# First layer of the token threes as 3x3 by 3x4 block products (29 of two units for 15 of four), and the threes' work issued in a list scheduler's order

## The chip, the cores and the metric

The kernel runs on one core of a Trainium2 chip. The metric is device time in microseconds: the median of several executions of the whole program.

## The reference

Sigmoid attention over 8 batches, 12 heads, 448 positions and head size 64, and then a feed-forward net with a squared ReLU over all 3584 tokens. All of it is float32.

```python
scores = scale * np.matmul(q, k.transpose(0, 1, 3, 2)) - np.log(S)
attn = 1.0 / (1.0 + np.exp(-scores))
x = np.matmul(attn, v)          # -> 3584 tokens x 768
h = x @ w_in                    # 768 x 2048
r = np.maximum(h, 0.0)
g = s * (r * r) + b
out = g @ w_out                 # 2048 x 768
```

## The kernel before

**Numbers.** Every matrix operand is split into a high part (rounded by ScalarE, `hi`) and a low part (the remainder, by VectorE, `lo`). A product is then three matmuls: high by high, high by low, low by high (`PARTS`).

**Three stages.** (1) Attention; beside it the weights of both layers are loaded as raw words and converted on VectorE and ScalarE, and the row sums of the first weight tiles of layer 2 are made. (2) *Token block 0* (512 of the 3584 tokens) goes through the net in the plain way, one tile of 128 hidden units after another (`order`: tiles 0, 8, 1, 9, ... 7, 15, sixteen iterations). Iteration i issues `ffn1` of its tile on TensorE, then the split of the next tile's weights (`base`), some of the weight sums, the activation (`activate`: four ScalarE operations, then the low part `g` on VectorE), and `ffn2` of the tile before it. So TensorE sees ffn1(i), ffn2(i-1), ffn1(i+1), ffn2(i), ..., and after the last ffn1 two ffn2 in a row. (3) The other six token blocks are taken in two *threes* of three blocks.

**The threes.** In a three, both layers are block matrix products computed with fewer multiplications than the plain way, from sums of blocks. Layer 1 multiplies 3 token blocks x 3 parts of the model width by 3 parts x 2 halves of the hidden width: 15 products instead of 18. Each product covers half the hidden width, as four *units* of 256 hidden columns; a unit is 12 matmuls of 128x512 (`L1095`). So layer 1 has 60 units per three, 720 matmuls, and layer 2 (`L1225`), also 15 products of four units, again 720. A product needs one operand from the tokens (`s_`, a sum of token tiles `a`, split into high and low on ScalarE and VectorE) and one *row* of the weights (a sum of weight blocks, split, stored in DRAM in `wd` during stage 2 and read back as `wu`, 512 KB for a unit). Results add up in four PSUM pairs or leave through ScalarE copies and VectorE additions.

**Row sums for layer 1** are made in stage 2 by `sums` (two row-sum groups of one hidden tile in each second iteration, eight sets of ten sums) and `sums_d`.

**Order.** Each engine runs its instructions in program order. All DMAs but two are issued by SyncE (SP) on one queue, in program order too. In the threes the order was written out by hand: tables `places`, `CHAINS_1`, `ORDER_2`, `early_jobs` and the due times `LATER_SUMS` say after which unit each sum, split and load is issued. The token tiles of the first three are loaded at the end of stage 2 in the order of `start`: 00, 20, 21 first, then 22 and 02, and the other four after the units 0 to 3.

**Memory.** Token sums, operands, results and hidden values live in equal 512 KB tiles, *slots*, of one heap (`Slots`): a freed slot goes to the back of a list and the next tile takes the one in front, so an instruction that fills a tile waits for the last reader of the slot's former content. Weight tiles wait in a roll of seven (`ROLL`).

Of the kernel before, what the change touches and what calls it, by code (L numbers as in the profile page):

```python
# [11 lines left out]
F32 = mybir.dt.float32  # L12
# [27 lines left out]
AHEAD = 6  # L40
# [5 lines left out]
LATER_SUMS = {  # L46
# [4 lines left out]
}  # L51
# [7 lines left out]
    (  # L59
# [4 lines left out]
    ),  # L64
    (
# [4 lines left out]
    ),  # L70
)

ROWS = (
    ("p", "q", "r", "u", "v", "w", "x", "y", "z", "d", "00", "10", "20", "01", "11"),
# [3 lines left out]
FIRST = {  # L78
# [3 lines left out]
}  # L82
SECOND = {
# [3 lines left out]
}  # L87

CHAINS_1 = ((4, 3), (10, 13, 2), (1, 8, 12), (7, 9, 11), (5, 0), (6, 14))
CHAINS_2 = ((8, 6, 7), (13, 10), (1, 5), (2, 4, 12), (3, 14, 9), (11, 0))  # L90
ORDER_2 = (8, 13, 6, 10, 7, 1, 2, 3, 5, 4, 11, 12, 14, 0, 9)
# [3 lines left out]
def sigmoid_attention_relu2_ffn(  # L95
# [19 lines left out]
    NPP = NP // 2  # L115
    NT = B * S // TB
# [14 lines left out]
    class Slots:  # L131


        def __init__(self, pl, n, tag):
            self.free_ = [(pl, f"{tag}{i}") for i in range(n)]
            self.at = {}

        def more(self, pl, n, tag):
            self.free_ += [(pl, f"{tag}{i}") for i in range(n)]

        def tile(self, shape, dtype, name):
            pl, tag = self.free_.pop(0)
# [4 lines left out]
        def free(self, t):  # L147
            _, pl, tag = self.at.pop(id(t))
            self.free_.append((pl, tag))
# [18 lines left out]
        [dram.tile([P, len(ROWS[l]), 2, 2 * KW], F32, name=f"wd_{l}_{p}") for p in range(NPP)]  # L168
        for l in range(2)
# [20 lines left out]
    for f in order:  # L190
        wf_tile(1, f, wfp_last if f % NP == NP - 1 else wfp)
        if f % NP < NP - 1:
            wf_tile(0, f, wfp)
# [27 lines left out]
    def block(l, f, n):  # L221

        third, hf = (int(n[0]), int(n[1])) if l == 0 else (int(n[1]), int(n[0]))
        return wf[l][f + hf * NP][:, third]
# [4 lines left out]
    def sums_ops(l, f, tl):  # L229
# [6 lines left out]
        def make(g):  # L236
            t = ts[g] = tl.tile([P, 3, 2, KW], F32R, name=f"t_{l}_{f}_{g}")
            k = 0
            for n, x, sign, y in SUMS[l][g]:
# [18 lines left out]
        def lo(g):  # L258
# [3 lines left out]
            def store():  # L262
# [4 lines left out]
                tl.free(t)  # L267

            if l:
                stores.append(store)  # L270
            else:
                store()
# [3 lines left out]
    def sums(l, f, tl):  # L276

        make, hi, lo = sums_ops(l, f, tl)
        make(0)
        make(1)  # L280
        yield
        hi(0)
        hi(1)
        yield
        make(2)
        lo(0)
        lo(1)
        yield
        hi(2)
        yield  # L290
        lo(2)
        yield

    def sums_d(l, p, tl):

        _, x, sign, y = SUMS[l][3]
# [7 lines left out]
        nc.sync.dma_start(wd[l][p][:, 9], f32(t).rearrange("p j h c -> p j (h c)"))  # L304
        tl.free(t)
# [11 lines left out]
    def base(l, f, t=None):  # L317
# [3 lines left out]
        hf, f = divmod(f, NP)  # L321
        thirds = [k for k in range(3) if (f"{k}{hf}" if l == 0 else f"{hf}{k}") in ROWS[l]]
        k0, k1 = thirds[0], thirds[-1] + 1
        row = ROWS[l].index(f"{k0}{hf}" if l == 0 else f"{hf}{k0}")
        nc.sync.dma_start(
            wd[l][f // 2][:, row : row + k1 - k0, f % 2],
            f32(t[:, k0:k1]).rearrange("p k h c -> p k (h c)"),
        )
        return t
# [157 lines left out]
    stores = []  # L487

# [163 lines left out]
    grps = ((0, 1), (2, 3))  # L652
    L1 = [(i, p) for c in CHAINS_1 for gr in grps for i in c for p in gr]
    L2 = [(i, p) for i in ORDER_2 for p in range(NPP)]
    stream = [(n, l, i, p) for n in range(len(threes)) for l in range(2) for i, p in (L1, L2)[l]]
    fetched = []

    def fetch():
        if len(fetched) < len(stream):
            n, l, i, p = stream[len(fetched)]  # L660
            t = roll.tile([P, 2, 2, KW], F32R, tag="wu", name=f"wu_{n}_{l}_{i}_{p}")
# [628 lines left out]
```

## Time and profile before

| | us |
|---|---|
| median of 3 runs (1038.56 to 1039.0) | 1038.66 |
| span of the profiled execution, first to last instruction | 1037.2 |
| TensorE matmuls busy | 1033.5 |
| VectorE busy | 837.3 |
| ScalarE busy | 617.0 |
| stage 1 / stage 2 / first three / second three, by the TensorE chain | 250.5 / 130.9 / 326.4 / 326.5 |

The profiled execution has no total of its own beside its span; the median of the runs lies 1.5 us above that span, which is the time around the first and the last instruction. The groups of the profile are read as: line, engine, operation, output<-input, shapes and count, then busy time, mean of one in ns, and the idle time of the engine just before them with what ended it. Lines are those of the kernel before; line 181 is the helper `sub` and line 178 the helper `add`, so tiles, not lines, tell which step an operation belongs to.

### The profile page before, as it was taken

The numbers are of one execution on the slowest core, as the hardware profiler recorded it, in microseconds if no ns is written. First come the engines' busy times: TensorE is split into PE (matmuls) and PEld (weight loads), VectorE is DVE, ScalarE is ACT, GpSimd is POOL, SyncE is SP. The second block draws the span as 40 slices with busy tenths as digits, with TensorE's granted clock in tenths as the row PEclk, the third lists the DMA queues.
The fourth block names the chain that finished last, engine by engine and source line by source line (L and its number), as shares of the span: only waits on it lengthen the run. The fifth ranks groups of instructions, "written<-read, shape, count | busy, mean of one in ns | idle before, by whom it ended". The sixth has DMA issues, their size and how long they took to land.

```text
span 1037.2 us, 13906 instructions
## 1 busy us (share of the span) xinstructions
PE 1033.5 (100%) x5290; PEld 780.9 (75%) x5290; DVE 837.3 (81%) x910; ACT 617.0 (59%) x666; POOL 0.2 (0%) x4
## 2 busy tenths in 40 slices
PE   9999999999999999999999999999999999999998
PEld 4545555555888888888888888888888888888887
DVE  5999999995988965898898897796455789888777
ACT  7999999988776755564445344344445335552432
POOL 0000000000000000000000000000000000000000
PEclk9999999999999999999999999999999999999999
DMA  9788989994999999999686676897666666676773
GB/s 334 265 333 340 359 321 393 345 398 190 338 362 366 358 409 410 340 341 322 201 267 190 218 230 219 292 317 249 197 192 194 194 192 196 191 233 212 221 227 119
DMA packets 101569, 287.17 MB, mean 277 GB/s; under 512 B 10240, under 2 KB 20352, under 8 KB 101504
## 3 DMA queue, kind: packets, MB, share of 16 engines
q1 hardware_dynamic: 101216, 285.84, 79.3%
q8 instruction: 42, 0.69, 0.3%
q10 hardware_dynamic: 288, 0.46, 0.1%
q14 instruction: 23, 0.19, 0.0%
HBM read 198.18 MB, written 88.08 MB: 276 GB/s over the span
## 4 chain that ended last, share of the span: by engine, by line
PE 100%; DVE 0%; issue 0%
PE o L1225 31%; PE h L1095 31%; PE pav L454 11%; PE psc L420 9%; PE ph L563 6%; PE po L765 6%; PE psc_l L441 2%; PE pav L463 2%; PE idle L482 0%; PE psc L426 0%; DVE C_t L181 0%
## 5 line engine op out<-in xcount | busy, mean ns | idle before, releaser
L1095 PE MATMUL h<-s_0h,wu 128*128 128x512 f32 x480 | 148.0, 389 | 0.0
L1095 PE MATMUL h<-s_1h,wu 128*128 128x512 f32 x480 | 147.8, 389 | 0.0
L400 ACT ACTIVATE a<-psc,nls 128x896 f32<-128x896 f32 x144 | 132.7, 1008 | 12.9 <-PE psc L420 10.1
L454 PE MATMUL pav<-a,v 128*64 128x448 f32 x576 | 113.8, 543 | 0.0
L1095 PEld LDWEIGHTS h<-s_0h,wu 128*128 128x128 f32 x480 | 90.1, 188 | 18.8
L1095 PEld LDWEIGHTS h<-s_1h,wu 128*128 128x128 f32 x480 | 90.1, 188 | 18.6
L968 ACT COPY G<-h 128x1024 f32<-128x1024 f32 x48 | 48.8, 1017 | 85.4 <-PE h L1095 57.7
L860 ACT ACTIVATE G<-G,b_sb,s_sb 128x1024 f32<-128x1024 f32 x48 | 59.8, 1246 | 61.4 <-DVE G L857 60.7
L1095 PE MATMUL h<-s_0l,wu 128*128 128x512 f32 x240 | 93.4, 389 | 0.0
L1095 PE MATMUL h<-s_1l,wu 128*128 128x512 f32 x240 | 93.4, 389 | 0.0
L454 PEld LDWEIGHTS pav<-a,v 128*64 128x64 f32 x576 | 39.1, 137 | 63.8 <-issue 45.4
L178 DVE TENSOR_TENSOR G<-G,h 128x1024 f32<-128x1024 f32 x40 | 48.8, 1219 | 39.1 <-PE h L1095 38.9
L1225 PE MATMUL o<-g_3h,wu 128*128 128x512 f32 (+1 forms) x244 | 79.0, 385 | 0.0
L1225 PE MATMUL o<-g_1h,wu 128*128 128x512 f32 x240 | 78.8, 389 | 0.0
L1225 PE MATMUL o<-g_2h,wu 128*128 128x512 f32 x240 | 78.8, 389 | 0.0
L1225 PE MATMUL o<-g_0h,wu 128*128 128x512 f32 x240 | 78.8, 389 | 0.0
L765 PE MATMUL po<-g,w 128*128 128x512 f32 x288 | 67.7, 389 | 0.0
L765 PEld LDWEIGHTS po<-g,w 128*128 128x128 f32 x288 | 54.1, 188 | 11.2
L563 PE MATMUL ph<-x0h,w 128*128 128x512 f32 x192 | 61.7, 390 | 0.0
L420 PE MATMUL psc<-qkh 64*128 64x448 f32 x284 | 54.8, 382 | 0.0
L1225 PEld LDWEIGHTS o<-g_3h,wu 128*128 128x128 f32 x244 | 45.6, 188 | 9.2
L1225 PEld LDWEIGHTS o<-g_0h,wu 128*128 128x128 f32 x240 | 45.1, 188 | 9.4
(152 smaller groups left out, 2029.7 us busy)
## 6 DMA issues: line engine op xcount, KB each, us to landing
wu<-wd SPq DMA_DIRECT2D x240, 512.0 KB, 3.8
wd<-t SPq DMA_DIRECT2D x36, 768.0 KB, 8.1
qk<-qk_t SPq DMA_DIRECT2D x23, 896.0 KB, 7.1
st<-w_out SPq DMA_DIRECT2D x16, 768.0 KB, 9.3
st<-w_in SPq DMA_DIRECT2D x16, 768.0 KB, 9.2
wd<-w SPq DMA_DIRECT2D x16, 768.0 KB, 5.9
v<-v_t SPq DMA_DIRECT2D x24, 448.0 KB, 5.4
xd<-xo SPq DMA_DIRECT2D x24, 448.0 KB, 4.4
```

The costliest lines, as they stand in the source:

```text
L178: nc.vector.tensor_tensor(o, x, y, op=ALU.add)
L400: nc.scalar.activation(a, psc[:, :, :S], AF.Sigmoid, bias=nls, scale=SCALE)
L420: nc.tensor.matmul(o[:, j, :S], two[wi][r, i, cols], two[xi][r, i, :S], start=m == 0, stop=m == 2,)
L441: nc.tensor.matmul(psc[half[i], j, :S], x[r, i, 1, 3 * P :], x[r, i, 0, :], start=True, stop=True,)
L454: nc.tensor.matmul(pav[r, i, :S], ld_[1][:, 3 * i + c, j, :], a[i, c][:, j, :], start=c == 0, stop=False,)
L463: nc.tensor.matmul(pav[r, i, :S], ld_[1][half[i], 6, j, :], a[half[i], j, :], start=False, stop=True,)
L563: nc.tensor.matmul(ph, w[:, k, wi, kc * P : (kc + 1) * P], x0[h][xi][:, cc, :], start=m == 0, stop=m == 3 * NCC - 1,)
L765: nc.tensor.matmul(pos[e], w[:, k, wi, kc * P : (kc + 1) * P], g[:, gi, :], start=first and i == 0, stop=last and i == 2,)
L860: nc.scalar.activation(x, x, AF.Identity, bias=b_sb, scale=s_sb)
L968: nc.scalar.copy(g(m, h), bk)
L1095: nc.tensor.matmul(bk[:, j], wt[:, j, wi, c * P : (c + 1) * P], opd[i][xi][:, c, :], start=i == ch[0] and m == 0, stop=m == 3 * KC - 1, sk ...
L1225: nc.tensor.matmul(o, wt[:, f, wi, e * P : (e + 1) * P], g[gi][:, f, tk], start=(end or i == ch[0] and p == 0) and f == 0 and m == 0, stop ...
```

## The change

**Layer 1 of a three** becomes a 3x3 by 3x4 block product. The hidden width is cut in four quarters instead of two halves; 29 products (`PRODUCTS_1`) of two units each take the place of 15 of four. Token sums come from `SUMS_1` (21 sums a three), weight rows from `ROW_SUMS` (25 sums, of which 20 are stored rows, and 9 stored plain blocks). Each product has its own operand split, and lists into which results it is added.

**Row sums** are made by `row_sums`: a list of small jobs (sum, `hi` of a tile of three rows, `lo` and its store) that the sixteen iterations work off by a budget, half of it ahead of `activate` and half behind.

**The threes** are no longer written out in order. Every operation becomes an `Op` of a `Planner` with an engine, an assumed time, its predecessors and a due time; `run` issues for each engine, in the order of its own clock, the most urgent one that can start. Layer 2 has the products as before. The planner also starts token loads (`FIRST_LOADS`: 01, 02, 00, 11 after iteration 12, then 12 and 20, the rest in planned order), places fetches, and stores.

```diff
-AHEAD = 6
+AHEAD = 7
+LATER_DUE = (40.0, 75.0, 110.0, 140.0)
+ROW_SUMS = (
+    ("t0", "01", -1, "03"),
+    ("t1", "12", -1, "13"),
...
+    ("t8", "10", 1, "12"),
...
+SUMS_1 = (
+    ("s0", "20", -1, "21"),
+    ("s1", "00", -1, "s0"),
+    ("s2", "s1", -1, "01"),
+    ("s3", "11", -1, "12"),
+    ("s4", "02", -1, "s3"),
+    ("s5", "s2", 1, "s4"),
...
+PRODUCTS_1 = (
+    ("01", 1, "12", 1, (("02", 1),)),
+    ("02", -1, "22", 0, (("02", -1),)),
+    ("s5", 1, "t8", 1, (("00", -1),)),
+    ("s7", -1, "t17", 0, (("12", 1),)),
+    ("s3", 1, "20", 3, (("00", 1), ("10", -1))),
...
+class Planner:
+    HOP = 0.2
...
+    def choose(self, todo, eng):
+        free, best = self.clock[eng], None
+        for o in todo[:1] if eng == "PE" else todo:
+            if any(d.end is None for d in o.after) or o.behind and o.behind.end is None:
+                continue
+            at = max([free] + [d.end + (self.HOP if d.eng != eng else 0.0) for d in o.after])
+            need = o.need() if callable(o.need) else o.need
+            if need:
+                slots = self.heap.free_
+                if len(slots) < (1 if o.late - at < 6.0 else 3):
+                    continue
+                at = max(at, slots[0][0], o.late - o.early)
+            if best is None or at < best[0] - 0.25:
+                best = at, o
...
+        return plan3.op("SP", 0.12, [], run, 1, early=30.0, lag=6.0)      # load_x, one token tile
...
+        plan3.op("SP", 0.06, [], run, late=10.0 + 5 * k, lag=4.0)         # first_out, block 0's results
...
-    sums_at = (0, 2, 4, 6, 8, 9, 11, 13)
-    sums_d_at = (2, 5, 9, 12)
+    row_jobs = [collections.deque(row_sums(f, cx)) for f in range(NQ4)]
+    cost = sum(w for w, _ in row_jobs[0])
+    before = NF - 4
+    shares = [(NQ4 - 1) * cost / before] * before + [cost / 3] * 4
...
     for i, f in enumerate(order):
         ph = ffn1(f, w1) if i else ph0
         if i + 1 < NF:
             w1 = base(0, order[i + 1])
...
+        rows_until(due + shares[i] / 2)
         g = activate(f, ph)
         if i + 1 < NF:
             w2[i + 1] = base(1, order[i + 1])
...
+        due += shares[i]
+        rows_until(due)
         if held:
             ffn2(*held, i == 1, False)
         held = (w2[i], g)
         if i == NF - 4:
-            load_raw(0, *start[0])
             early.close()
             roll = pool(ctx, "roll", ROLL, side="right")
-            heap.more(pool(ctx, "h1", 1, side="right"), 14, "r")
-            for m, k in start[1:3]:
-                load_raw(0, m, k)
+            heap.more(pool(ctx, "h1", 1, side="right"), 12, "r")
+            start(FIRST_LOADS[:4])
             for _ in range(4):
                 fetch()
         if i == NF - 3:
-            for m, k in start[3:5]:
-                load_raw(0, m, k)
-            fetch()
+            start(FIRST_LOADS[4:6])
...
-    heap.more(pool(ctx, "h2", 1), 31, "l")
+    heap.more(pool(ctx, "h2", 1), 32, "l")
...
+    plan3.clock.update(PE=0.0, DVE=0.0, ACT=1.5, SP=-2.0)
+    plan3.run()
```

**Where instructions move: token block 0, ScalarE.** The rows are ScalarE's, of the kernel before, around the activation `r_14` of iteration 13 (`t_0_6_2` and `td_0_3` are tiles of weight rows, `w_` are split weights).

```order
L314 CAST w_0_7_3592<-wf_0_7_2710 128x3x256
L256 CAST t_0_6_2_3508<-t_0_6_2_3508 128x3x256
L301 CAST td_0_3_3517<-td_0_3_3517 128x2x256
L754 ACTIVATE r_14_3609<-ph_14_3573 128x512
L755 ACTIVATE r_14_3609<-r_14_3609 128x512
```

The same place after.

```order
L471 CAST t_0_3_1_3511<-t_0_3_1_3511 128x3x256
L540 CAST w_0_7_3599<-wf_0_7_2708 128x3x256
L471 CAST t_0_3_2_3530<-t_0_3_2_3530 128x3x256
L471 CAST t_0_3_3_3605<-t_0_3_3_3605 128x3x256
L1266 ACTIVATE r_14_3615<-ph_14_3580 128x512
L1267 ACTIVATE r_14_3615<-r_14_3615 128x512
```

The two casts ahead of `r_14` (`t_0_6_2`, `td_0_3`) were of sums made in an earlier iteration; the two right ahead of it now (`t_0_3_2`, `t_0_3_3`) are of sums that VectorE makes in the same stretch.

VectorE at that place, before: from the `g` of iteration 12 to that of iteration 13.

```order
L181 TENSOR_TENSOR g_6_3520<-r_6_3521,g_6_3520 128x512
L181 TENSOR_TENSOR w_1_14_3527<-wf_1_14_129,w_1_14_3527 128x3x256
L181 TENSOR_TENSOR w_0_7_3592<-wf_0_7_2710,w_0_7_3592 128x3x256
L181 TENSOR_TENSOR t_0_6_2_3508<-t_0_6_2_3508 128x3x256
L178 TENSOR_TENSOR t_0_7_0_3600<-wf_0_7_2710,wf_0_15_2711 128x256
L178 TENSOR_TENSOR t_0_7_0_3600<-wf_0_15_2711,t_0_7_0_3600 128x256
L178 TENSOR_TENSOR t_0_7_0_3600<-wf_0_7_2710,t_0_7_0_3600 128x256
L181 TENSOR_TENSOR t_0_7_1_3604<-wf_0_15_2711,t_0_7_0_3600 128x256
L178 TENSOR_TENSOR t_0_7_1_3604<-wf_0_7_2710,t_0_7_1_3604 128x256
L181 TENSOR_TENSOR t_0_7_1_3604<-wf_0_15_2711 128x256
L181 TENSOR_TENSOR g_14_3608<-r_14_3609,g_14_3608 128x512
```

VectorE after, the second half of the same stretch (ahead of these rows, behind `g_6`, come one `w` split, five row sums, the `lo` of `t_0_3_1` and another `w` split).

```order
L355 TENSOR_TENSOR t_0_3_2_3530<-wf_0_11_116,wf_0_15_2709 128x256
L355 TENSOR_TENSOR t_0_3_3_3605<-wf_0_7_2708,wf_0_11_116 128x256
L352 TENSOR_TENSOR t_0_3_3_3605<-wf_0_7_2708,t_0_3_3_3605 128x256
L355 TENSOR_TENSOR t_0_3_3_3605<-t_0_3_3_3605,t_0_3_2_3530 128x256
L352 TENSOR_TENSOR t_0_3_4_3610<-t_0_3_2_3530,t_0_3_3_3605 128x256
L355 TENSOR_TENSOR t_0_3_3_3605<-t_0_3_3_3605 128x3x256
L355 TENSOR_TENSOR g_14_3614<-r_14_3615,g_14_3614 128x512
```

The `lo` of `t_0_3_3` (second to last row) needs that tile's cast on ScalarE, and the cast needs the sums just above it; before, no `lo` in this stretch belonged to sums made in the same stretch.

**Where instructions move: the SP queue between stage 2 and the first three.** Before, from the first token load on.

```order
L337 DMA a_0_00_3549<-xd_1_84 128x2x384
L337 DMA a_0_00_3549<-xd_2_85 128x2x128
L337 DMA a_0_20_3559<-xd_3_86 128x2x256
L337 DMA a_0_20_3559<-xd_4_87 128x2x256
L337 DMA a_0_21_3562<-xd_3_86 128x2x256
L337 DMA a_0_21_3562<-xd_4_87 128x2x256
L663 DMA wu_0_0_4_0_3565<-wd_0_0_91 128x1024
L663 DMA wu_0_0_4_1_3567<-wd_0_1_92 128x1024
```

After, around the load of the same token tile 21 (the first token load, of tile 01, stands 31 DMAs ahead of it).

```order
L478 DMA wd_0_1_92<-t_0_3_4_3610 128x3x512
L478 DMA wd_0_1_92<-t_0_3_6_3697 128x2x512
L894 DMA wu_4_3768<-wd_0_0_91 128x1024
L894 DMA wu_5_3770<-wd_0_1_92 128x1024
L894 DMA wu_6_3772<-wd_0_0_91 128x1024
L1345 DMA out_t<-o_4_3810 128x2x512
L1345 DMA out_t<-o_2_3813 128x2x512
L1345 DMA out_t<-o_0_3816 128x2x512
L565 DMA a_0_21_3829<-xd_3_86 128x2x256
L565 DMA a_0_21_3829<-xd_4_87 128x2x256
```

Tile 21 moved behind the last row stores, three more weight fetches and the three result stores of token block 0.

VectorE then works on the first three in this order after the change (`o_0_0_k` are the operands of product k, `s` token sums).

```order
L355 TENSOR_TENSOR o_0_0_0_Nonel_3778<-a_0_01_3560,o_0_0_0_Noneh_3774 128x1024
L944 SCALAR_TENSOR_TENSOR o_0_0_1_Nonel_3780<-a_0_02_3563,o_0_0_1_Noneh_3776 128x1024
L355 TENSOR_TENSOR s3_0_0_None_3827<-a_0_11_3569,a_0_12_3649 128x1024
L355 TENSOR_TENSOR s4_0_0_None_3838<-a_0_02_3563,s3_0_0_None_3827 128x1024
L355 TENSOR_TENSOR o_0_0_4_Nonel_3855<-s3_0_0_None_3827,o_0_0_4_Noneh_3840 128x1024
L355 TENSOR_TENSOR a_0_20_3652<-a_0_20_3652,a_0_21_3829 128x1024
L355 TENSOR_TENSOR s1_0_0_None_3875<-a_0_00_3566,a_0_20_3652 128x1024
L355 TENSOR_TENSOR s2_0_0_None_3894<-s1_0_0_None_3875,a_0_01_3560 128x1024
L352 TENSOR_TENSOR s2_0_0_None_3894<-s2_0_0_None_3894,s4_0_0_None_3838 128x1024
L355 TENSOR_TENSOR s6_0_0_None_3912<-a_0_10_3832,a_0_12_3649 128x1024
L355 TENSOR_TENSOR o_0_0_2_Nonel_3922<-s2_0_0_None_3894,o_0_0_2_Noneh_3914 128x1024
```

The operand of product 2 (last row), which units 4 and 5 read, stands behind four operations that follow each other from the load of tile 21; before, the first products read tiles 00, 20 and 21.

More of the change, by code (lines that the diff above doesn't have):

```diff
@@ L167, in sigmoid_attention_relu2_ffn @@
     wd = [
-        [dram.tile([P, len(ROWS[l]), 2, 2 * KW], F32, name=f"wd_{l}_{p}") for p in range(NPP)]
-        for l in range(2)
+        [dram.tile([P, len(ROWS[l]), 2, 2 * KW], F32, name=f"wd_{l}_{p}") for p in range(n)]
+        for l, n in enumerate((NQ4 // 2, NPP))
     ]
@@ L267, in store @@
                 tl.free(t)
-            if l:
-                stores.append(store)
-            else:
-                store()
-        return make, hi, lo
[L276 to L292, printed above, removed]
+                kept.update((l, r, f) for r in ROWS[l][3 * g : 3 * g + 3])
@@ new lines, in sigmoid_attention_relu2_ffn, with __init__, use, sum_op @@
+    plan3 = Planner(heap)
+    banks, held_by, used_at, open_ = {}, [[] for _ in range(4)], [-1] * 4, {}
+    units = []
+    class Value:
+        def __init__(self, uses=0):
+            self.uses, self.t = uses, None
+    def use(v, at):
+        v.uses -= 1
+        if not v.uses and v.t is not None:
+            heap.free(v.t, at)
+            v.t = None
+    def sum_op(o, x, sign, y, after, name):
+        def run(at):
+            xt, yt = x.t, y.t
+            if x.uses == 1:
+                o.t, x.t = x.t, None
+            elif y.uses == 1:
+                o.t, y.t = y.t, None
+            else:
+                o.t = slot(name)
+            op(o.t, xt, sign, yt)
+            use(x, at)
+            use(y, at)
+        return plan3.op("DVE", 1.22, after, run, lambda: int(x.uses > 1 and y.uses > 1), early=EARLY)
@@ new lines, in split, with run_hi, run_lo @@
+    def split(v, sign, after, uses, name):
+        hi, lo = Value(uses), Value(uses)
+        def run_hi(at):
+            hi.t = slot(name + "h", True)
+            if sign > 0:
+                nc.scalar.copy(hi.t, v.t)
+            else:
+                nc.scalar.activation(hi.t, v.t, AF.Copy, scale=-1.0)
+        def run_lo(at):
+            lo.t = slot(name + "l", True)
+            if sign > 0:
+                sub(lo.t, v.t, f32(hi.t))
+            else:
+                nc.vector.scalar_tensor_tensor(
+                    lo.t, v.t, -1.0, f32(hi.t), op0=ALU.mult, op1=ALU.subtract
+                )
+            use(v, at)
+        h = plan3.op("ACT", 1.06, [after], run_hi, 1, early=EARLY)
+        return (hi, lo), [h, plan3.op("DVE", 1.22, [h], run_lo, 1, early=EARLY)]
@@ new lines, in stored, with run, load_x @@
+    def stored(n, res, end):
+        for c, (v, ops) in res.items():
+            if c == end:
+                continue
+            def run(at, c=c, v=v):
+                m, k = int(c[0]), int(c[1])
+                out_store(v.t, KC * k, threes[n][m], KC)
+                use(v, at + 5.0)
+            plan3.op("SP", 0.06, ops, run, lag=4.0, late=(len(units) + 5) * UNIT)
+    def load_x(n, m, k):
+        v = Value()
+        def run(at):
+            v.t = slot(f"a_{n}_{m}{k}")
+            load_tokens(v.t, threes[n][m], KC * k, KC)
+        return v, plan3.op("SP", 0.12, [], run, 1, early=30.0, lag=6.0)
@@ new lines, in first_out, with run @@
+    def first_out(k):
+        def run(at):
+            out_store(outs[k], evict[2 * k], 0, 2)
+            heap.free(outs[k], at + 5.0)
+        plan3.op("SP", 0.06, [], run, late=10.0 + 5 * k, lag=4.0)
+    for k in range(3):
+        first_out(k)
+    plan3.deadlines()
+    FIRST_LOADS = []
+    for a, *_ in PRODUCTS_1:
+        seen = [a]
+        while seen:
+            x = seen.pop(0)
+            d = {s_[0]: (s_[1], s_[3]) for s_ in SUMS_1}.get(x)
+            if d:
+                seen += d
+            elif x not in FIRST_LOADS:
+                FIRST_LOADS.append(x)
@@ L751, in activate, with start @@
+    def start(names):
+        for x in names:
+            o = loads[0][x, None][1]
+            plan3.now(o, -20.0)
     def activate(f, ph):
@@ L824, in sigmoid_attention_relu2_ffn @@
         if i == NF - 3:
-            for m, k in start[3:5]:
-                load_raw(0, m, k)
-            fetch()
-        if i == NF - 2:
-            for _ in range(5, AHEAD):
-                fetch()
-    for q_ in (4, 3):
-        for fn in todo.pop(q_):
-            fn()
+            start(FIRST_LOADS[4:6])
+    assert not row_jobs
+    for _ in range(4, AHEAD):
+        fetch()
+    plan3.clock.update(DVE=-6.0, ACT=-6.0)
+    plan3.run(lambda o: o.first)
     ffn2(*held, False, True)
```

938 lines of the change are left out of this document (464 added, 474 removed), and 50 rows, old and new, of tables (FIRST, LATER_SUMS, PRODUCTS_1, SECOND).

## The prediction

> **What bounds the kernel now.** I read the head of the page first, then the chain of waits in order of time, then the windows of each stage, then the waits.
>
> ```profile
> span 1037.2 us, 13906 instructions
> PE 1033.5 (100%) x5290; PEld 780.9 (75%) x5290; DVE 837.3 (81%) x910; ACT 617.0 (59%) x666; POOL 0.2 (0%) x4
> PE 100%; DVE 0%; issue 0%
> ```
>
> The third line is the chain's share by engine: TensorE works from end to end, so only two things move the time, TensorE's own work and new gaps in it. The chain in order of time (start, length, what) gives the stages:
>
> ```profile
> 336.47 4.08 PE ph L563 x18
> 340.55 4.08 PE po L765 x18
> 365.03 4.08 PE po L765 x18
> 373.19 8.16 PE po L765 x36
> 544.55 163.20 PE o L1225 x720
> 707.75 163.20 PE h L1095 x720
> 870.95 163.28 PE o L1225 x726
> ```
>
> The first three starts at 373.19 + 8.16 = 381.35. A layer of a three is 720 matmuls in 163.20 us, 0.2267 us each; one of 60 units takes 2.72. In token block 0, 18 matmuls (one `ffn1` or `ffn2`) take 4.08. The windows (start and end, length, busy time of TensorE, its weight loads, VectorE, ScalarE, GpSimd with counts, granted clock, DMA share, GB/s) say how much room the others have:
>
> ```profile
> 250.00:381.40 131.40, 131.40 (x585) 108.44 (x578) 107.42 (x178) 88.07 (x126) 0.00 (x0) 1.00 0.93 350
> 381.40:544.60 163.20, 163.20 (x721) 135.18 (x720) 133.80 (x142) 88.97 (x97) 0.00 (x0) 1.00 0.88 318
> 544.60:707.70 163.10, 163.10 (x721) 135.10 (x720) 138.51 (x122) 69.88 (x69) 0.00 (x0) 1.00 0.74 240
> 360.00:410.00 50.00, 50.00 (x223) 41.40 (x222) 28.73 (x32) 29.57 (x38) 0.00 (x0) 1.00 1.05 406
> ```
>
> VectorE is 82 to 85% busy, ScalarE 43 to 67%: no engine but TensorE is full over a stage. The last line is another matter: from 360 to 410 us, on both sides of the border between block 0 and the first three, the DMA engines are never free and move 406 GB/s. Whatever is added or put later there lands later.
>
> **Term A, the products: -10.9 us.** 29 products of two units are 58 units in place of 60, in both threes: 2 x 2 x 2.72 = 10.88 us, 48 matmuls. Every matmul lies on the chain, so all of it counts.
>
> **The added work of VectorE and ScalarE as a mean load: 0.** Operand splits go from 30 to 58 in the two threes, token sums from 30 to 42, evictions by VectorE from 98 to 118, and the squares of the hidden values go partly to ScalarE (40 to 16). On VectorE that is 442 operations of 1024 columns for 417, at most 1.22 us each, some 30 us more in 642; on ScalarE 80 more at about 1.06, 85 us.
>
> ```profile
> L181 DVE TENSOR_TENSOR s_0l<-a,s_0h 128x1024 fp32r<-128x1024 f32 x9 | 11.0, 1221 | 5.8 <-ACT s_0h L678 4.3 <-DMA a<-xd 1.5
> L678 ACT CAST s_0h<-a 128x1024 fp32r<-128x1024 f32 x9 | 9.5, 1055 | 4.8 <-DMA wd<-t_u 4.8
> L181 DVE TENSOR_TENSOR t<-t 128x768 fp32r<-128x768 f32 x36 | 33.3, 952 | 0.0
> L256 ACT CAST t<-t 128x768 fp32r<-128x768 f32 x36 | 29.1, 829 | 1.8 <-DVE t L178 1.5 <-DVE t L181 0.3
> L181 DVE TENSOR_TENSOR w<-wf,w 128x768 fp32r<-128x768 f32 x32 | 29.9, 954 | 3.8 <-ACT w L314 3.5
> L178 DVE TENSOR_TENSOR t<-wf,t 128x256 f32<-128x256 f32 x36 | 15.3, 424 | 1.0
> ```
>
> That leaves VectorE below 90% and ScalarE below 65% in the threes. The cover is this idle time; where a single operand is late it does not help, which is what the terms below are about. The row sums in block 0 (100 instead of 88 sums at 0.42, 5 us of VectorE in a stage where it idles 131.4 - 107.4 = 24) are covered as a mean too.
>
> **Term C, block 0, iterations 12 to 15: +6.0 us (0 to 9).** The last set of rows needs the weight tiles that come last, so its ten sums, casts and splits are squeezed into three iterations. In the new order ScalarE's casts of row tiles stand ahead of the activation `r_14`, and wait for sums that VectorE makes in that same stretch; VectorE's `lo` and `g_14` then wait for ScalarE. So the engines stop running beside each other: from one `g` to the next, the loop is the sum of VectorE's work up to the last cast's sums, that cast, and the activation. The activation (ScalarE's four operations, then `g` on VectorE) is read from the timeline before:
>
> ```profile
> 365.07 0.60 ACT L754 ACTIVATE r<-ph 128x512 f32<-128x512 f32 x1 [2.45 <-PE ph L563]
> 367.21 0.62 ACT L757 CAST g<-r 128x512 fp32r<-128x512 f32 x1
> 367.87 0.69 DVE L181 TENSOR_TENSOR g<-r,g 128x512 fp32r<-128x512 f32 x1 [1.67 <-ACT g L757]
> 344.71 0.69 DVE L181 TENSOR_TENSOR g<-r,g 128x512 fp32r<-128x512 f32 x1
> 352.92 0.68 DVE L181 TENSOR_TENSOR g<-r,g 128x512 fp32r<-128x512 f32 x1
> ```
>
> From 365.07 to the end of the cast at 367.83 are 2.76 us. Iteration 12 to 13, from the rows of the new order: `g` 0.69, two `w` at 0.95, ten sums at 0.42, two row `lo` at 0.95, twice about 0.4 of waiting for a cast of 0.83 that a VectorE operation half covers, and the chain of 2.76 less the `lo` of 0.95 beside it: 11.3, or 11.0 as back-to-back operations overlap by 0.09 (344.71 + 0.69 is 345.40, the next starts at 345.31). The stretch before it counts to the same 11, the one behind it (iteration 13 to 14, one `w` fewer ahead of the last cast) to 9.5, the last (one `w`, two sums, casts of 0.83 and 0.62, the chain) to 6.7. TensorE's pace is 8.16 for each iteration, 4.08 for the last, since two `ffn2` follow each other there.
>
> What it can stand: `g` may come 8.16 - 2.76 - 0.69 = 4.7 us after its earliest time before `ffn2` is late. Before, iteration 11 was 1.4 late (344.71 against 340.55 + 2.76 = 343.31). I keep that start and add 11.0 - 8.16 = 2.8 twice: 1.4 + 5.6 = 7.0, over 4.7 by 2.3. That is the gap ahead of `ffn2` of iteration 13; then 9.5 - 8.16 = 1.3, then 6.7 - 4.08 = 2.6, of which I count 2.4 since its first cast may be done early. Sum 6.0. The lower end, 0, is that ScalarE's casts are early enough for the engines to overlap as before; the upper, 9, takes each loop one cast wait (0.83) longer, four times.
>
> **Term B, the fifth unit of the first three: +10.0 us (1.5 to 13).** Product 2 needs `s5`, which needs token tile 21. Before, tile 21 is the third load behind iteration 12; now the last row stores, seven weight units and three result stores of block 0 come first on SP's queue. From the first token load through tile 21 the new order has 21 pieces of 512 KB (7 token tiles, 7 weight units, 3 results, 4 stores) and 5 stores of 768 KB: 21 x 0.524 + 5 x 0.786 = 14.9 MB. At 0.405 MB/us, just under the 406 GB/s above, that is 36.9 us.
>
> ```profile
> wd<-w SPq DMA_DIRECT2D x16, 768.0 KB, 5.9
> wd<-t SPq DMA_DIRECT2D x36, 768.0 KB, 8.1
> wu<-wd SPq DMA_DIRECT2D x240, 512.0 KB, 3.8
> 354.91 4.44 SPq L337 DMA_DIRECT2D a<-xd  x6
> ```
>
> The last column is the median time from issue to landing; the last row is the timeline's, the first token loads before, at 354.91. Now they stand behind a row store whose `lo` comes 4.7 us after `g_6` (0.69, `w` 0.95, three sums, cast wait, `lo`); `g_6` comes at 352.92 + 2.8 = 355.7, so they go out at 360.4. The store just ahead adds 0.79 MB, 1.9 us, and a weight unit's 3.8 us less its bytes' 1.3 leaves 2.5 of latency. Tile 21 lands at 360.4 + 1.9 + 36.9 + 2.5 = about 401.7, say 401. The operand then takes four operations of 1.22 on VectorE (a20 - a21, `s1`, `s2` and the last sum; the order beside the change shows them), a cast of 1.06 and the `lo` of 1.22: 7.2, so 408.2. The fifth unit would start at 381.35 + 6.0 + 4 x 2.72 = 398.2. TensorE stands for 10.0 us. If the queue is not what counts and tile 21 only waits for the result stores of block 0 (`ffn2` ends at 387.4, a copy, then a load of 3.8 to 6.6), it lands 393 to 396 and the wait is 1.5 to 4.3; if reads and writes slow each other to 0.375 MB/us, 36.9 becomes 39.8 and the wait 13. I take the queue, since the row at 406 GB/s is of this very stretch.
>
> **Term D, slots in layer 2: +1.7 us (0 to 5).** The heap is one slot smaller (12 + 32 for 14 + 31 in the diff). By the order of instructions, the operand of unit 92 (first three) is split into a slot that unit 91 frees: 1.22 - 0.23 = 1.0; in the second three a `lo` stands third behind an operation that waits for unit 193's slot, 3 x 1.22 - 2.72 - 0.23 = 0.7. A dozen other units have 0.9 to 1.6 us to spare by the same count; four of them falling short by 0.8 is the upper end.
>
> **Term E, slow matmuls behind the gap: +1.7 us (0 to 3.1).** The trace's only matmuls behind an idle TensorE are its first:
>
> ```profile
> 0.77 3.15 PE L482 MATMUL idle<-const-bfloat16-1.0 128*128 128x448 bf16 x8 [0.77 <-PEq L1280]
> ```
>
> 394 ns for 448 columns, 0.88 ns a column, against 226.7 / 512 = 0.443 later. If half rate lasts as long behind a gap of 10 us as there, 3.15 us do the work of 1.57; I take 1.7 for the one long gap, nothing for the short ones; twice that if the iteration gaps also trip it, 0 if it belongs to the program's start. The Trainium skill, "TensorE: Matmul & The Clock Gate", in "Part 1: The HAM clock gate (the "warmup" mystery)", says that an idle window of about 3.4 us halves the rate until about 3.4 us of busy time. By it the term would be 1.7 (an estimate); the first row agrees with the half rate, and no row here shows it behind a gap, where the granted clock of every window reads 1.00.
>
> **Sum:** -10.9 + 6.0 + 10.0 + 1.7 + 1.7 = +8.5 us. The profiled execution before spans 1037.2 and the median of the runs is 1038.66, 1.5 more, which stays: 1038.7 + 8.5 = 1047.2.
>
> **Rivals.**
> - *Block 0 is covered, the token tile alone waits.* VectorE has 24 us idle there, which speaks for it; the casts in the new order against it. The loads then go out at 354.9, tile 21 lands at 354.9 + 1.9 + 36.9 + 2.5 = 396.2, the operand is ready at 403.4, the unit's time is 392.2: a wait of 11.2. -10.9 + 11.2 + 1.7 + 1.7 = +3.7: 1042.4. The two waits trade against each other, which makes the sum less sensitive than either.
> - *The token tile is in time (the other side).* If small tile loads get ahead of the stores, or the queue has more room than 406 GB/s, tile 21 lands before 398.2 - 7.2 = 391.0 and only C and D are left, -10.9 + 6.0 + 1.7 = -3.2; with C small as well, 1028 to 1030. With D at 1.7 and C at 6.0 it decides at a wait of 3.2, a landing before 394. That asks for 14.9 MB in 29 us, 0.51 MB/us, which no stretch shows; a token load took 6.6 us at the least there:
>
> ```profile
> DMA to landing us min/median/max: 6.6/7.8/9.7
> ```
>
>  That speaks against it. The Trainium skill, "DMA: Bandwidth & Descriptors", in "Queues, rings and completion order", says completion is not first in, first out for an issuing engine; the row's spread of 3 us is what it could give here.
> - *The small waits multiply.* Late operands push evictions and slots: four more units of 2 us each, or half rate behind every gap: +8 on top, 1055.
>
> **How the numbers follow.** The forecast .55; block 0 covered .20; tile in time .13, of which .10 end over 2 us faster; small waits multiply .12. About 0.2%, 2 us, can be told from no change. Faster: .10, and .05 of the covered case, where B is under 7; same: .03 of the tile in time, .02 each of the forecast and the covered case; slower the rest, .78. The likeliest case has 1042 to 1052 (B from 5 to 13, C 3 to 9, which trade). The range reaches to 1037 on the faster side, short of the case that C and B both vanish, and to 1054, into half the last case; .10 and .06 are left out below and above, and some .02 of the covered case.
>
> **What the profile after would show.** 5242 matmul records or a few less, `h` in 58 units; TensorE idle ahead of `po` in the last three iterations, released by VectorE's `g`, with ScalarE waiting for VectorE ahead of `r`; one gap of about 10 us some 11 us into the first three, and VectorE waiting for a DMA of `a` there; matmuls at twice their time behind it; gaps of 1 us in layer 2. It is wrong if the fifth unit starts with no gap (tile 21 landed by 391), if `ffn2` never waits, or if gaps stand at other units, which I have not costed.

## The result, and the profile after

The changed kernel takes 1051.98 us (median of four executions, 1051.13 to 1055.8), the kernel before 1038.83 in the same session: a ratio of 1.0132 (95% interval 1.0115 to 1.0149), 13.2 us slower. The forecast was 1047.2, in a range of 1037 to 1054. The profiled execution is the longest of the four, with a span of 1053.6 us against 1037.2, 16.4 more; the terms below are read from it, and one of them is smaller in the other executions.

The head of the page after:

```profile
span 1053.6 us, 13919 instructions
PE 1030.4 (98%) x5242; PEld 774.1 (73%) x5242; DVE 866.8 (82%) x945; ACT 690.4 (66%) x746; POOL 0.2 (0%) x4
PE 83%; DVE 5%; ACT 5%; DMA 5%; issue 2%; SPq 0%; DVEq 0%; ACTq 0%
```

48 matmuls are gone, and the chain is no longer TensorE alone: 17% of it now leads through other engines and DMAs. The chain in order of time (start, length, what) shows where:

```profile
369.70 12.50 DMA wd<-w
382.26 9.28 DMA wd<-w
391.60 10.76 DMA out_t<-o
402.42 5.37 DMA wu<-wd
...
409.99 1.21 DVE o_Nonel L355
411.24 149.28 PE b L983 x647
560.52 92.27 PE b L992 x407
652.88 1.24 DVE o_2l L944
654.16 70.81 PE b L992 x311
724.96 157.76 PE b L983 x696
882.72 46.25 PE b L992 x204
929.36 6.48 DMA out_t<-r
935.94 1.24 DVE o_3l L944
937.22 110.47 PE b L992 x479
```

From 370 to 408 the chain is a row of DMAs, one behind the other: row stores, block 0's results, a weight unit. (That unit is not what VectorE waited for: VectorE works from 403.79 on without a pause until the operand is done.) Layer 1 of the second three (724.96, 696 matmuls in 157.76 us) runs without a gap. TensorE's own waits, from its timeline (in brackets the idle time before, and what ended it; the second row is the first unit of the threes, which before stood at 381.19):

```profile
382.69 0.50 PE L1277 MATMUL po<-g,w 128*128 128x512 f32 x1 [1.56 <-ACT g L1269]
387.44 0.39 PE L983 MATMUL b<-o_Noneh,wu 128*128 128x512 f32 x1
409.98 0.79 PE L983 MATMUL b<-o_Noneh,wu 128*128 128x512 f32 x1 [11.50 <-ACT o_Noneh L935]
411.24 0.80 PE L983 MATMUL b<-o_Nonel,wu 128*128 128x512 f32 x1 [0.46 <-DVE o_Nonel L355]
403.79 1.23 DVE L355 TENSOR_TENSOR a<-a,a 128x1024 f32<-128x1024 f32 x1 [13.36 <-DMA a<-xd]
```

The 11.5 us stand ahead of the fifth unit, and the last row is the reason: VectorE's first sum with tile 21 had waited 13.4 us for that tile, which landed at 403.8. Behind the gap the matmuls are slow. The windows (columns as in the prediction) of the gap, and of a second one at 935:

```profile
402.00:405.00 3.00, 0.00 (x0) 0.00 (x0) 1.21 (x1) 0.00 (x0) 0.00 (x0) 0.60 1.09 397
411.00:414.00 3.00, 2.76 (x7) 2.18 (x8) 3.00 (x4) 2.14 (x3) 0.00 (x0) 0.50 0.12 48
414.00:417.00 3.00, 3.00 (x10) 2.40 (x9) 3.00 (x4) 0.66 (x1) 0.00 (x0) 0.62 0.00 0
417.00:420.00 3.00, 3.00 (x15) 2.50 (x14) 2.93 (x4) 2.20 (x3) 0.00 (x0) 1.00 0.62 183
936.00:940.00 4.00, 2.78 (x9) 2.28 (x10) 3.97 (x4) 1.06 (x1) 0.00 (x0) 0.82 0.30 114
940.00:944.00 4.00, 4.00 (x15) 3.18 (x15) 3.15 (x3) 1.06 (x1) 0.00 (x0) 0.76 0.42 125
```

The granted clock falls to 0.50 about 4 us into the idle time (0.60 over 402 to 405 is full speed until 402.6) and comes back at 416.3, 6.3 us after TensorE's restart.

The account, from the starts of the stages (block 0 from its first matmul at 250.46 before and 250.61 after):

| step | forecast | measured in the profiled execution |
|---|---|---|
| A, 48 matmuls fewer | -10.9 | -10.9 |
| C, block 0 | +6.0 | +6.1 (136.83 for 130.73) |
| B, gap at the fifth unit | +10.0 | +12.0 (11.50 + 0.46) |
| E, half clock behind it | +1.7 | +3.3 (560.52 - 387.44 is 15.3 over 157.76, less the 12.0) |
| D, layer 2 of the first three | +1.0 | +1.2 (164.44 for 163.20) |
| D, layer 2 of the second three | +0.7 | +4.6 (170.88 for 166.25) |
| sum | +8.5 | +16.3 of 16.4 |

The gap behind D in the second three, 2.60 us ahead of 937.22, is VectorE's: its `lo` waits for a result store to land.

```profile
935.94 1.23 DVE L944 SCALAR_TENSOR_TENSOR o_3l<-s,o_3h 128x1024 fp32r<-128x1024 f32 x1 [1.74 <-DMA out_t<-r]
```

### The profile page after: what moved, and what is told of

It is laid out like the page before. It is cut to its first block, busy times and chain, and to the rows that moved or that the text cites. A ratio compares the mean times of both kernels' runs of the same rounds, so it can differ in the third digit from the quotient of the medians.

```text
span 1053.6 us, 13919 instructions
## 1 busy us (share of the span) xinstructions
PE 1030.4 (98%) x5242; PEld 774.1 (73%) x5242; DVE 866.8 (82%) x945; ACT 690.4 (66%) x746; POOL 0.2 (0%) x4
## 4 chain that ended last, share of the span: by engine, by line
PE 83%; DVE 5%; ACT 5%; DMA 5%; issue 2%; SPq 0%; DVEq 0%; ACTq 0%
PE b L992 30%; PE b L983 29%; PE pav L682 11%; PE psc L648 9%; DMA wd<-w 3%; PE psc_l L669 2%; DVE w L355 2%; PE pav L691 2%; DVE t L355 2%; ACT w L540 1%; DMA out_t<-o 1%; ACT t L471 1%; ACT r L1268 1%; ACT r L1267 1%; DMA out_t<-r 1%
## 5 line engine op out<-in xcount | busy, mean ns | idle before, releaser
L983 PE MATMUL b<-o_Noneh,wu 128*128 128x512 f32 x928 | 288.0, 391 | 11.5 <-ACT o_Noneh L935 11.5
L983 PEld LDWEIGHTS b<-o_Noneh,wu 128*128 128x128 f32 x928 | 175.4, 189 | 48.2 <-ACT o_Noneh L935 11.9
L983 PE MATMUL b<-o_Nonel,wu 128*128 128x512 f32 x464 | 181.6, 391 | 0.5 <-DVE o_Nonel L355 0.5
L352 DVE TENSOR_TENSOR r<-r,b 128x1024 f32<-128x1024 f32 x58 | 70.0, 1217 | 41.4 <-PE b L992 17.2
L983 PEld LDWEIGHTS b<-o_Nonel,wu 128*128 128x128 f32 x464 | 87.7, 189 | 19.4 <-DVE o_Nonel L355 1.0
L355 DVE TENSOR_TENSOR r<-r,b 128x1024 f32<-128x1024 f32 x60 | 72.7, 1217 | 30.6 <-PE b L992 16.7
L992 PE MATMUL b<-o_0h,wu 128*128 128x512 f32 x240 | 79.0, 390 | 0.0
L992 PE MATMUL b<-o_2h,wu 128*128 128x512 f32 x240 | 78.8, 389 | 0.0
L992 PE MATMUL b<-o_1h,wu 128*128 128x512 f32 x240 | 78.7, 389 | 0.0
L992 PE MATMUL b<-o_3h,wu 128*128 128x512 f32 x232 | 77.0, 393 | 0.0
L1116 ACT ACTIVATE r<-r,b_sb,s_sb 128x1024 f32<-128x1024 f32 x48 | 59.1, 1240 | 11.4 <-DVE r L1113 10.9
```

Of the source, the lines that this page charges most:

```text
L352: nc.vector.tensor_tensor(o, x, y, op=ALU.add)
L355: nc.vector.tensor_tensor(o, x, y, op=ALU.subtract)
L983: nc.tensor.matmul(bk[:, j], wt[:, j, wi, c * P : (c + 1) * P], tiles[xi][:, c, :], start=first and m == 0, stop=m == 3 * KC - 1, skip_gro ...
L992: nc.tensor.matmul(bk[:, e], wt[:, f, wi, e * P : (e + 1) * P], tiles[gi][:, f], start=first and f == 0 and m == 0, stop=p == np_ - 1 and ...
L1116: nc.scalar.activation(v.t, v.t, AF.Identity, bias=b_sb, scale=s_sb)
```

## The experiments

Each is the changed kernel with one edit, or several where it says so; the kernel before ran on the same chip.

**Tiles 21 and 10 early.**

```diff
-            start(FIRST_LOADS[4:6])
+            start(FIRST_LOADS[4:8])
```

> The changed kernel, but token tiles 21 and 10 are loaded with the two of iteration 13 instead of behind the result stores of block 0. Theory (the fifth unit waits for tile 21 only because 6.5 MB of stores, weight units and results stand ahead of it on SP's queue): tile 21 lands some 16 us earlier, about 388, and the gap of 11.5 us ahead of the fifth unit goes, with the half-clock stretch behind it (3 us): 1037 to 1040 us, and less than 1.5 us of TensorE idle between the first and the tenth unit. Rival (the gap is four VectorE operations and two of the split in a row, or the weight row of product 2 is late as well): wu_4 or the operand still arrives late, the gap shrinks to 5 to 8 us, 1045 to 1048.

Measured: 1041.15 us (1039.03 to 1042.95), ratio to the kernel before 1.0023 (1.0011 to 1.0034), 10.8 less than the changed kernel. Tile 21 lands at 387.5, the fifth unit has two waits of 0.3 and 0.6 us instead of the gap, and the clock stays at 1.00 there. What TensorE waits for in the profiled execution, which is one of the slower ones (1042.9):

```profile
PE b L992 <- DVE o_3l L944: 3.9, 2, 2.7
PE po L1277 <- ACT g L1269: 3.1, 3, 1.5
PE po L1277 <- DVE g L355: 0.7, 3, 0.2
PE b L983 <- DVE o_Nonel L355: 0.6, 1, 0.6
PE b L983 <- DVE r L352: 0.5, 1, 0.5
PE b L983 <- DMA wu<-wd: 0.3, 1, 0.3
```

Terms B and E are the place of these loads on SP's queue, shown. The time missed the expected 1037 to 1040 by 1: 1.4 us of small waits remain among the first units, where I had asked for less than 1.5, and the two gaps in layer 2 (3.9 together, and behind the longer one the clock falls as in the changed kernel).

**Casts behind the activation, in block 0.** `hi` and `lo` of a tile of rows are set aside and issued behind the next activation and weight split (a job of weight below 0 is a `hi`, one of 0.95 a `lo`, with which the store of the rows goes too).

```diff
-                    jobs.append((0, lambda g=g: hi(g)))
+                    jobs.append((-1, lambda g=g: hi(g)))
...
-            fn()
+            if w < 0 or w == 0.95:
+                behind.append(fn)
+            else:
+                fn()
...
             w2[i + 1] = base(1, order[i + 1])
+        for fn in behind:
+            fn()
+        behind.clear()
```

> The changed kernel, but in token block 0 each cast and lo of a tile of weight rows is issued behind the next activation and weight split instead of at once. Theory (ScalarE's casts ahead of the activation wait for VectorE's sums, and make the loop serial): TensorE no longer waits ahead of ffn2 of iterations 13 to 15, block 0 shrinks from 136.8 to 131.5 or less, the first three starts at 382. Since the loads of the token tiles then go out earlier by less than that, the gap at the fifth unit grows by 0 to 5: 1046 to 1052. Rival (block 0 is longer because VectorE has more work in its last iterations): block 0 stays at 136 or more.

Measured: 1053.06 us (ratio 1.0136, 1.0112 to 1.0161). From its timelines and waits:

```profile
380.97 0.39 PE L983 MATMUL b<-o_Noneh,wu 128*128 128x512 f32 x1
356.72 6.51 SPq L565 DMA_DIRECT2D a<-xd  x8
403.00 1.23 DVE L355 TENSOR_TENSOR a<-a,a 128x1024 f32<-128x1024 f32 x1 [9.74 <-DMA a<-xd]
PE b L983 <- ACT o_Noneh L935: 17.2, 1, 17.2
```

Block 0 is back at 130.73 us, exactly its time before, with no wait ahead of any `ffn2`: term C was the order of ScalarE's casts and of the `lo` behind them, which the edit moves together, shown. But the time did not fall. The first token loads went out 4.2 us earlier (356.72; 360.96 in the changed kernel), and tile 21 landed 0.8 us earlier (403.00 for 403.79): nearly all of the 6 us went into the gap, 17.2 for 11.5. My upper end, 1052, was too low by 1.

**The fourth unit four times, then five times.** The repeated matmuls start the sum again each time, so they change no result; in the second kernel the factor ahead of `(u == 3)` is 4.

```diff
-                for j in range(2):
+                for j in [0, 1] * (1 + 3 * (u == 3)):
```

> The changed kernel, but the 12 matmuls of the fourth unit of the first three are issued four times, each time from the start of the sum, so that TensorE works 8.2 us longer in the gap ahead of the fifth unit. Theory (the gap costs its length and then a stretch at half clock of some 3 us of loss): 8.2 us of added work cost nothing, the granted clock stays at 1.00 there, and the time falls by about 3 us to 1048 to 1050. Rival (what follows the gap is slow for another reason, a late operand each time): the time is the same or up to 2 us longer, 1052 to 1054.

Measured: 1052.38, the rival's number. The added 8.2 us cost nothing, but nothing was won either. The reason is not the rival's: a gap of 3.4 us was left, and the clock fell in it all the same, so that the theory was not put to the test. The next kernel leaves no gap.

> As the kernel with the fourth unit issued four times, but five times, 10.9 us of added work, so that less than 1 us of the gap stays. With 8.2 us of work a gap of 3.4 stayed, the granted clock fell to 0.50 all the same, and the 647 matmuls behind took 149.1 us as with the gap of 11.5. Theory (any gap of some us costs the same half-clock stretch, none costs nothing): the clock stays at 1.00, those matmuls take 146.7, the time falls by 2 to 3 us to 1048 to 1050. Rival (they are slow for another reason): 149 again and 1051 to 1054.

Measured: 1051.94. With 10.9 us added the clock stays up. The 647 matmuls behind the gap, in the chain of the first kernel (gap 3.4 us) and of the second (none):

```profile
411.39 149.08 PE b L983 x647
```
```profile
410.69 146.95 PE b L983 x647
```

147 us against 149.1 (149.28 with the gap of 11.5): the slow matmuls are the clock's, 2.3 us of the 3.3, and they cost the same after 3.4 us of idle time as after 11.5. The total stayed in the rival's range. In the profiled execution layer 1 of the first three is indeed shorter, 169.1 us (388.54 to 557.64) for 173.1, but block 0 took 138.4 for 136.8, and the second three's gap was 2.5 us. The windows show what happened in block 0: behind its last wait for `g`, 1.5 us, the granted clock fell here, which it did not do in the changed kernel.

```profile
383.00:385.00 2.00, 2.00 (x6) 1.59 (x7) 1.84 (x2) 1.55 (x3) 0.00 (x0) 0.62 1.08 401
385.00:387.00 2.00, 2.00 (x7) 1.54 (x6) 1.91 (x3) 1.17 (x2) 0.00 (x0) 0.53 1.05 409
```

Half speed from 383.5 to 386.9 is 1.7 us of loss, about the 1.6 by which block 0 was longer. The edit cannot be its cause, since the added matmuls come later. The claim rests on the stretch, not on the total.

**Block 0's results stored later.**

```diff
-        plan3.op("SP", 0.06, [], run, late=10.0 + 5 * k, lag=4.0)
+        plan3.op("SP", 0.06, [], run, late=60.0 + 5 * k, lag=4.0)
```

> The changed kernel, but the planner gives the three result stores of block 0 a due time 50 us later, so that they stand behind the token tiles. Theory (bytes ahead on the queue set the landing of tile 21): 1.57 MB fewer ahead of it, 3.9 us, and no wait of SP for the end of block 0: the gap shrinks from 11.5 to 6 to 8, time 1045 to 1048. Rival (tile 21 waits for the row stores alone, whose sums end late): the gap stays within 2 us of 11.5, 1050 to 1053.

Measured: 1053.49. The planner issued the same order on SP's queue with the new due time as with the old one, so this was a second look at the changed kernel and says nothing of the stores. The look is of use: the gap at the fifth unit is 11.2 us again, but the one in the second three only 1.0 us, with the clock at 1.00 behind it, and that layer takes 167.7 us, not 170.9. That part of term D differs from execution to execution. And the medians of the same program, 1051.98 and 1053.49, differ by 1.5 us: so small a difference between two of these kernels says nothing.

**Slots in the order of their time.** A stored result is taken to free its slot after 9 us, and the free list is sorted.

```diff
             self.free_.append((when, pl, tag))
+            self.free_.sort(key=lambda x: x[0])
...
-                use(v, at + 5.0)
+                use(v, at + 9.0)
```

> The changed kernel, but the heap's free list is kept in the order of the time at which a slot comes free, and a stored result is taken to free its slot 9 us after its store is issued instead of 5. Theory (the gap of 2.6 us in layer 2 of the second three is a slot whose result store had not landed): that gap goes, and in the execution shown the half-clock stretch behind it, so the last layer of the second three takes 163 to 165 us instead of 168: 1047 to 1050, with less spread from run to run. Rival (the lo is late for VectorE's own order): the gap stays at 2 us or more there, 1051 to 1054.

Measured: 1049.28 (1048.59 to 1049.93), ratio 1.0100 (1.0086 to 1.0114): 2.7 under the changed kernel, below every one of that program's eight executions (1051.13 at the least), and with a spread of 1.3 instead of 4.7. Its chain has layer 2 of the first three in one piece, and no gap in the second:

```profile
560.77 163.20 PE b L993 x720
723.97 157.76 PE b L984 x696
881.73 160.48 PE b L993 x708
```

The store that the changed kernel waited for, `out_t<-r` at 929.36, took 6.5 us where its planner had assumed 5. Term D was slots, shown; which of the edit's two lines removed which gap is open.

**The first two edits together.**

> Both edits at once: token tiles 21 and 10 loaded with those of iteration 13, and the casts and lo of row tiles in block 0 issued behind the next activation. Theory (the landing of tile 21 was what ended both waits, so block 0's 6 us came back as a longer gap; with the landing out of the way they count): 1041.15 less 5.5 to 6, 1035 to 1036, block 0 in 131. Rival (the row stores, issued later, now hold the weight units 4 to 6 instead, and block 0's gain turns into a wait for wu): 1039 to 1042.

Measured: 1044.13 (ratio 1.0050, 1.0034 to 1.0065), slower than tile 21 alone by 3 and above both ranges, although block 0 takes 130.7. The rival's kind of answer, in a place nobody had named: 9.9 us ahead of the second unit.

```profile
PE b L983 <- ACT o L1364: 9.9, 1, 9.9
```

**All three edits.**

> All three edits: tiles 21 and 10 early, row casts behind the activation, slots in order of their time. Theory (three separate waits, each of which had eaten a part of the 10.9 us that the products save): 1041.15 - 5.9 (block 0) - 3 to 4.6 (second three) = 1030 to 1032.5, faster than the kernel before by 6 to 8. Rival (a new order of the planner brings waits of its own at other units, or the weight units become late): 1034 to 1038.

Measured: 1041.03 (ratio 1.0019, 1.0010 to 1.0028), above both ranges, with the same 9.9 us and no gap in layer 2 over 0.2 us. ScalarE's timeline in this kernel:

```profile
391.48 0.59 ACT L1364 COPY o<-po 128x512 f32<-128x512 f32 x1 [11.78 <-DMA wd<-t]
```

The copy that empties block 0's PSUM banks writes into a slot whose memory held a tile of row sums, and that tile's store, issued later now, is still on the full queue. The second unit needs one of those banks. I then gave the slots another order.

```diff
+    early_ = [12, 13, 14, 2, 3, 6, 7, 8, 9, 15, 20, 21, 22, 31, 28, 0, 1, ...]
+    l_ = heap.free_[-32:]
+    heap.free_[-32:] = [l_[i] for i in early_]
```

> As the kernel with all three edits, but the 32 slots that come free at the end of block 0 are used in another order: those whose memory no late row store still reads come first. Theory (the 9.9 us ahead of the second unit there were ScalarE's copy of block 0's results into a slot whose former tile, a tile of row sums, was still being stored on the full queue): that wait goes; the next to be late is the weight unit or the operand of the fifth unit, by 2 to 5 us and up to 2.3 of half clock: 1032 to 1036. Rival (the queue as a whole is what ends the stretch, whoever waits for it): TensorE waits some 8 to 10 us at the fifth unit instead and the time stays at 1039 to 1042.

Measured: 1041.43, with the 9.9 us in the same place. The edit was void: a slot gets its memory at its first use, so the new first slot took the old place. A repeat, no evidence for the rival.

**Stores of layer 2's rows later**, two of them (tiles 7 and 15, 1.3 MB; the edit missed the third that the expectation counts).

```diff
+        if l and f in (NP - 1, NF - 2, NF - 1):
+            put_off.append(store)
...
     ffn2(*held, False, True)
+    for fn in put_off:
+        fn()
```

> As the kernel with the slots in the other order, and the last three stores of layer 2's plain weight rows (2.1 MB, not read before layer 2) issued behind block 0's last matmul instead of ahead of and among the row stores. Theory (on a full queue only what must land early should stand early): row stores and weight units 4 to 6 land 5 us earlier, the wait at the fifth unit goes: 1028 to 1032, 7 to 11 faster than the kernel before. Rival (bytes put off there only delay the units behind): another unit among the first twelve waits as long, 1033 to 1038.

Measured: 1037.51 (ratio 0.9985, 0.9976 to 0.9994), in the rival's range. The wait at the second unit is 6.7 us instead of 9.9: 3.2 us for 1.3 MB, which is what 406 GB/s make of them.

**The slots' memory in the other order**, and then the tiles' loads too.

```diff
+    for _, pl_, tag_ in l_:
+        pl_.tile([P, 2, TB], F32, tag=tag_, name=f"none_{tag_}")
```

> As the kernel with the later w_1 stores (two of them, of tiles 7 and 15, 1.3 MB), but now the slots' memory is laid out first and then taken in the other order, so that ScalarE's copies of block 0's results no longer go into memory that a late row store reads (in the two kernels before, the memory of a slot was laid out at its first use, so the changed order had moved no memory). Theory: the 6.7 us ahead of the second unit go, with the 2.5 of half clock behind them; six sums stand between the landing of tile 21 at 384.1 and the operand of the fifth unit, so that one waits 3 us and perhaps 2.3 of half clock come back: 1031 to 1034. Rival (the queue itself ends the stretch): a weight unit of the first twelve waits 6 to 8 instead, 1036 to 1038.

```diff
+    FIRST_LOADS[:8] = ["01", "02", "20", "21", "00", "11", "12", "10"]
```

> As that kernel, with the eight token tiles loaded in the order 01, 02, 20, 21, 00, 11, 12, 10, so that only four sums stand behind the last landing. Theory: the operand of the fifth unit is there at 390.5, before the unit's time of 392: no wait, no half clock, 1028.5 to 1031.5, 8 to 10 under the kernel before. Rival (the weight unit of product 2, whose row stores stand right ahead of it, is what lands last): the time stays within 1.5 us of that kernel's.

Measured: 1037.27 and 1037.24 (both 0.9986, 0.9977 to 0.9995 and 0.9978 to 0.9995). The rivals won. The copies wait no longer, and TensorE waits for weight units. Of the first kernel, two rows of TensorE's timeline and one of SP's:

```profile
394.68 0.47 PE L990 MATMUL b<-o_Noneh,wu 128*128 128x512 f32 x1 [2.83 <-DMA wu<-wd]
406.88 0.77 PE L990 MATMUL b<-o_Noneh,wu 128*128 128x512 f32 x1 [3.76 <-DVE a L356]
397.20 1.11 SPq L901 DMA_DIRECT2D wu<-wd  x1
```

The fifth unit waits for its weights; the eighth waits too. The profile puts that down to a VectorE operation which this unit does not need; its weight unit, issued at 397.20 behind the results and tile 22, took 9.5 us to land, which is 406.7 and fits. These two lie 1.6 us under the kernel before, and so did the kernel ahead of them: taking the wait at the second unit away gained nothing, it came back at the fifth and the eighth. For all three the interval excludes no change by little, and the gain is less than the 0.2% that I took as the bound.

Where the first layer of the first three ends, in three kernels with waits in different places (tile 21 early; the slots' memory; the load order):

```profile
547.38 95.21 PE b L992 x420
```
```profile
547.32 84.33 PE b L999 x372
```
```profile
547.14 84.33 PE b L999 x372
```

In the first, block 0 ends 6 us later than in the other two. With the stretch from 381 on free of waits it would be 539. That the same bytes through one queue set this end is my reading of the three, and it is not shown: no kernel here has fewer bytes in the stretch, and the kernel with the first two edits, whose bytes are those of the first, ends this layer at 551.61.

## Why the prediction came out right, step by step

The time lies in the range, 4.8 us above the forecast. The waits came where they were named, except the one that a store caused in the second three; B, E and D all came out larger than their terms, so nothing cancelled, and it was the width of the range that held the sum.

**The bound, and term A: right.** Two layers of 58 units, 157.76 us where there is no gap.

**Term C: right in mechanism and size** (6.1 for 6.0), shown by the kernel with the casts behind the activation. From one `g` to the next (345.02, 355.95, 366.75, 376.22, 382.67 in the changed kernel) the loop took 10.9, 10.8, 9.5 and 6.5 us; 11, 11, 9.5 and 6.7 were forecast. The sum of VectorE's and ScalarE's rows along the loop was enough to get it. One sign was off: most of TensorE's idle time ahead of `po` ends with ScalarE's cast of `g` (3.1 us), and only 0.7 with VectorE's `g`.

**Term B: right mechanism, 2 us short.** The fifth unit's time came at 398.5 (398.2 forecast); tile 21 landed at 403.8, not 401, and the operand then took 7.4 us (7.2). Bytes over rate gave the landing to 3 us in 43; the term that was off is the rate, 386 GB/s over 361 to 403.8 and not 405, which makes 38.7 us of the 36.9.

**Term E: mechanism right, mis-sized.** 1.7 assumed that the clock comes back after the 3.15 us of the program's first matmuls. It took 6.3 us after the restart. The Trainium skill, "TensorE: Matmul & The Clock Gate", in "Part 1: The HAM clock gate (the "warmup" mystery)", gives one busy window of about 3.4 us for the recovery. The second gap's windows agree with that (0.82 and 0.76 are half speed from 938.5 to 941.9); behind the first gap it took longer, since the interval in which TensorE restarted did not count (the last section has the working).

**Term D: 1.7 forecast, 5.8 measured,** the step that failed most. The unit in the first three was the one named (0.94 us idle, 1.0 forecast). In the second three I had read the order of instructions for engines that free a slot, and passed over a slot that a result *store* frees: 2.6 us of gap, and 1.9 of half clock behind it, which I had excluded for short gaps.

**The rival "block 0 is covered": its sum was wrong.** It moved the landing of tile 21 forward with the issue of the first load and got 1042.4. The kernel with the casts behind the activation is that case: its loads went out 4.2 us earlier, the landing came 0.8 earlier, the time was 1053. On this full queue an earlier issue was not an earlier landing; the bytes ahead count, and more row stores stood ahead: three of them, not one, were issued right before the first load, and ten stores, not nine, stand between it and tile 21. By the same token terms B and C were not separate prices: taking C away alone bought nothing.

**The rival on the other side** did not occur: tile 21 was not in time, and only moving its load brought it there.

## What to carry to other kernels

A scheme with fewer matmuls can need its operands sooner: before, the operands of the first eight units were made of three token tiles, now of eight, while the loads stand among stores on a queue that is already full. Here the work that was saved on the bound engine was not worth its time, and would be only if every DMA in that stretch can move forward too; count the bytes ahead of each first use on the queue, not only the issue time. And look at each slot or buffer that a store frees: it is free when the store has landed, and that took longest just where the queue was full (a median of 11.7 us for block 0's three result stores, 6.5 for the one at 929).

## What the runs showed of the hardware that I had not expected

The clock's drop does not follow the length of a gap. 3.4 us of idle time cost as much half clock as 11.5; 2.6 to 2.8 us in the second three brought a drop in four kernels (479 matmuls in 110.3 to 110.5 us), 2.5 us brought none in one (108.87), and 2.8 us ahead of the fifth unit none in the kernel with the slots' memory laid out first. The gaps of up to 1.6 us in block 0 brought none in most kernels, and one of 1.5 us did in one (the fourth unit five times). In the second three the drop came 1.3 us after the restart (937.2, half speed from 938.5), so it hit running matmuls.

What the traces follow is a grid in time. The 16 stretches at half clock in the changed kernel and the twelve runs last 3.41 us (seven of them), 6.83, 10.24, 13.65 or 20.48, all multiples of 3.41, and where one execution has two, their starts lie 157 or 159 times 3.41 apart. Cut each execution into intervals of 3.41 us that end where its clock falls. After every interval with 2.1 us or more of idle TensorE the clock was at half; after those with 1.5 or less it never fell; with 1.8 it fell in one kernel and not in another. It came back only after an interval with at most 0.3 us idle, and not after those with 0.85 or more. The gap of 2.6 us in the changed kernel left 2.1 us of one interval idle (935.1 to 938.5), while the gap of 2.5 us that brought no drop lay across a border, 1.3 us on one side and 1.2 on the other. Term E follows from the same reading: at the restart at 409.98 the interval to 412.9 had 1.0 us idle and did not count, the next one was full, and the clock came back at its end, 416.3. The reading is made of these traces after the fact, and no run was built to test it.
